# Column units gathered behind the row stage, one ring of five PSUM banks, a reordered start and zero products ahead of it

## The chip, the cores and the metric

The kernel runs on one core of one Trainium2 chip. Its time is device microseconds of one execution, taken as the median of several. The five engines of the core run their own instruction streams in order: TensorE (PE for matmuls, PEld for weight loads), VectorE (DVE), ScalarE (ACT), GpSimd (POOL) and SyncE (SP), which here only issues DMAs. An engine waits for another through semaphores.

## The reference

```python
# x: (8, 4224, 192), weight: (8 heads, 7 taps)
w = softmax(weight)                                  # per head
out = einsum('hk,bskhg->bshg', w, windows_of_7(x))   # causal convolution, one filter per head of 24 channels
# then, on that result x:
gate = sigmoid(sum_k conv_w[k] * shifted(x, k))      # causal, 5 taps per channel
val = x @ w_val                                      # 192 x 192
result = (gate * val) @ w_out                        # 192 x 192
```

## The kernel before

The tokens of the eight sequences are laid out as two long streams. They are cut into eleven groups `g`; `NJS` says how many windows of 122 tokens a group has per row (2, 4, eight times 6, and 2 at the end). A group is cut into column blocks of up to 458 tokens: the 39 steps `n` of the main loop. Steps 0 and 1 belong to group 0, steps 2 to 4 to group 1, and from step 5 on each full group has four steps.

**Column stage** (`conv_unit`, L277 and L286). The first convolution is a matmul: a load of input (`x<-xw`, one head of one group) is the stationary operand, `band` (a banded matrix of the softmaxed taps) the moving one. One unit is three or four of these matmuls into one PSUM bank `pc`, a ScalarE copy into a row buffer `e`, and, when the head of that group is complete, `conv_scatter`: DMAs that bring the rows into the channel-major tiles `x1` (channels 0 to 127, heads 0 to 4 and a part of 5; L303) and `x2` (channels 128 to 191, the rest of head 5 and heads 6 and 7; L318, four DMAs for one head). A full group has 16 units.

**Row stage**, per step `n`, on `x1` and `x2`:
- the gate: `gate_open` (ScalarE, L340) puts the first tap into the PSUM tiles `pa` (two banks) and `pb` (one bank), `gate_taps` (VectorE, L347) adds four more taps, `gate_close` (ScalarE, L360) writes the sigmoid to `g1` and `g2`. This runs one to two steps ahead.
- `split` (ScalarE casts L368 and L376, GpSimd subtractions L369 and L377) makes a high and a low half (`xh`, `xl`) of each operand, `split_gated1` and `split_gated2` the same (`ph`, `pl`) for the gated product.
- the product with `w_val`: `chunk1` (L398 to L400), `chunk21` (L408, 64 rows), `chunk12` (L415, 64 columns, float32), `chunk2` (L424), accumulated in `pv`. `gated(n, q)` (VectorE, L446) multiplies it with the gate: q = 0 and 1 are the halves of the first 128 channels, q = 2 the rest.
- the product with `w_out` for the step before (`o = n - 1`), the same four pieces into `po`, then `project` (ScalarE copies L461, one DMA per step).

The eight PSUM banks: `pa` 2, `pb` 1, four in turn for `pv` and `po`, and one, `ps_c`, for all column units. The order on every engine is the order in which the code is written (`manual_schedule`). In a step the column units stand in four places, `conv(c[0])` to `conv(c[3])`, one unit in each for a step with four; `due[n]` says how many must have been done. The beginning decodes the two weight matrices from 64-bit words on VectorE (`make`, L198 to L214; `low`, L244), does seven column units ahead of step 0, ten in step 0, five in step 1 and six in step 2, then four a step up to step 30 and one a step from 31 to 34.

## Time and profile before

| | us |
|---|---|
| median of three runs | 428.06 (427.2 to 428.23) |
| the profiled execution | 426.18 |
| span of its profile | 424.4 |
| matmuls busy (PE) | 387.3 (91%) |
| VectorE busy (DVE) | 351.4 (83%) |
| ScalarE busy (ACT) | 327.3 (77%) |
| GpSimd busy (POOL) | 235.5 (55%) |

The profile is of one execution. A row of the timeline begins with the start and the length in us; "x6" counts instructions that were merged into one row (a float32 matmul shows as two instructions, so a unit of three is x6), and the brackets say how long the engine had stood idle and what ended that. In a table of windows each engine has its busy time and, as x, its number of instructions. "SPq" is SyncE's instruction stream.

### The profile page before, as it was taken

What the parts mean: (1) busy time and instruction counts of PE and PEld (TensorE: products, weight loads), DVE (VectorE), ACT (ScalarE), POOL (GpSimd) and SP (SyncE); (2) the same over time, 40 slices, a digit from 0 to 9 for tenths busy, and PEclk for the clock granted to TensorE, in tenths of its full rate; (3) what the DMA queues carried; (4) which work ended last, traced back from release to release, by engine and by line L of the source; (5) the groups of instructions that cost most, each with busy time, mean ns of one, the idle gap of its engine ahead of it and who ended that gap; (6) DMA issues with size and microseconds to landing.
All of it is one profiled execution on the core that took longest, in us unless ns stands there. A gap on an engine that the chain in (4) does not pass through costs nothing.

```text
span 424.4 us, 7773 instructions
## 1 busy us (share of the span) xinstructions
PE 387.3 (91%) x2683; PEld 308.6 (73%) x2683; DVE 351.4 (83%) x466; ACT 327.3 (77%) x580; POOL 235.5 (55%) x170
## 2 busy tenths in 40 slices
PE   3437787999999999999999999999999999999897
PEld 3336666888877877777887888887787777776574
DVE  4855357799999899999998989999989998999980
ACT  4253466888888888888888888888888889888772
POOL 1322144565556666665666665556666666765770
PEclk9855899999999999999999999999999999999999
DMA  7572588788877788877877866887887766222313
GB/s 284 158 220 61 159 187 223 218 215 221 209 238 215 219 213 227 214 206 207 237 217 191 236 205 204 200 234 233 211 214 232 214 175 179 101 89 90 133 68 138
DMA packets 30819, 81.59 MB, mean 192 GB/s; under 512 B 4764, under 2 KB 9612, under 8 KB 30780
## 3 DMA queue, kind: packets, MB, share of 16 engines
q1 hardware_dynamic: 30524, 80.87, 67.8%
q8 instruction: 21, 0.34, 0.4%
q0 software_dynamic: 256, 0.24, 0.2%
q14 instruction: 18, 0.15, 0.1%
HBM read 28.85 MB, written 26.00 MB: 129 GB/s over the span
## 4 chain that ended last, share of the span: by engine, by line
PE 74%; DVE 10%; ACT 5%; DMA 4%; SPq 3%; issue 3%; POOL 1%; DVEq 0%; ACTq 0%; POOLq 0%
PE pc L277 23%; PE pv L415 7%; PE pv L408 6%; PE pv L424 6%; PE po L415 5%; PE po L408 5%; PE po L424 4%; DVE pa L347 4%; DVE pb L347 4%; PE po L398 3%; PE po L399 3%; PE po L400 3%; PE pv L398 3%; PE pv L399 3%; PE pv L400 3%
## 5 line engine op out<-in xcount | busy, mean ns | idle before, releaser
L347 DVE SCALAR_TENSOR_TENSOR pa<-x,cwt,pa 128x912 f32<-128x912 f32 (+6 forms) x156 | 175.4, 1124 | 23.4 <-ACT pa L340 16.1
L277 PEld LDWEIGHTS pc<-band,x 128*120 128x120 f32 x816 | 102.2, 186 | 30.2 <-ACT e L286 24.2
L277 PE MATMUL pc<-band,x 128*120 128x122 f32 x816 | 115.8, 279 | 7.6 <-ACT e L286 7.3
L286 ACT COPY e<-pc 120x366 f32<-120x366 f32 (+1 forms) x144 | 68.2, 475 | 68.8 <-PE pc L277 56.1
L347 DVE SCALAR_TENSOR_TENSOR pb<-x,cwt,pb 128x456 f32<-128x456 f32 (+6 forms) x156 | 105.0, 673 | 4.1
L369 POOL TENSOR_TENSOR pl<-g,ph 128x912 fp32r<-128x912 f32 (+5 forms) x38 | 79.2, 2085 | 50.2 <-ACT ph L368 50.2
L377 POOL TENSOR_TENSOR pl<-g,ph 128x456 fp32r<-128x456 f32 (+5 forms) x38 | 43.3, 1140 | 104.4 <-ACT ph L376 104.4
L446 DVE TENSOR_TENSOR g<-pv,g 128x456 f32<-128x456 f32 (+6 forms) x117 | 67.5, 604 | 31.9 <-PE pv L408 25.4
L369 POOL TENSOR_TENSOR xl<-x,xh 128x912 fp32r<-128x912 f32 (+6 forms) x39 | 71.2, 1826 | 15.9 <-ACT xh L368 15.9
L461 ACT COPY ot<-po 128x456 f32<-128x456 f32 (+6 forms) x117 | 57.5, 529 | 10.3 <-PE po L408 4.8
L415 PE MATMUL pv<-x,wvf 128*64 128x228 f32 (+6 forms) x312 | 37.8, 364 | 3.2 <-ACT ot L461 1.9
L398 PE MATMUL pv<-xh,wvh 128*128 128x456 f32 (+6 forms) x78 | 31.1, 399 | 10.2 <-ACT xh L368 10.2
L340 ACT ACTIVATE pa<-x,cwt 128x912 f32<-128x912 f32 (+6 forms) x39 | 38.8, 994 | 0.9 <-DMA x<-e 0.7
L377 POOL TENSOR_TENSOR xl<-x,xh 128x456 fp32r<-128x456 f32 (+6 forms) x39 | 39.3, 1007 | 0.0
L368 ACT CAST ph<-g 128x912 fp32r<-128x912 f32 (+5 forms) x38 | 36.1, 949 | 2.1 <-DVE g L446 2.1
L360 ACT ACTIVATE g<-pa 128x912 f32<-128x912 f32 (+6 forms) x39 | 35.7, 915 | 2.0 <-DVE pa L347 1.7
L368 ACT CAST xh<-x 128x912 fp32r<-128x912 f32 (+6 forms) x39 | 35.6, 914 | 0.0
L415 PE MATMUL po<-g,wof 128*64 128x228 f32 (+5 forms) x304 | 34.8, 349 | 0.0
L398 PE MATMUL po<-ph,woh 128*128 128x456 f32 (+5 forms) x76 | 30.8, 406 | 0.2 <-DVE g L446 0.2
L400 PE MATMUL pv<-xl,wvh 128*128 128x456 f32 (+6 forms) x78 | 28.6, 367 | 0.7 <-POOL xl L369 0.7
L399 PE MATMUL pv<-xh,wvl 128*128 128x456 f32 (+6 forms) x78 | 28.5, 365 | 0.0
L415 PEld LDWEIGHTS pv<-x,wvf 128*64 128x64 f32 x312 | 19.0, 138 | 12.5 <-ACT ot L461 2.8
(81 smaller groups left out, 580.1 us busy)
## 6 DMA issues: line engine op xcount, KB each, us to landing
x<-xw SPq DMA_DIRECT2D x64, 360.0 KB
out<-ot SPq DMA_DIRECT2D x24, 684.0 KB
x<-e SPq DMA_DIRECT2D x40, 343.1 KB
out<-ot SPq DMA_DIRECT2D x8, 687.0 KB
x<-e SPq DMA_DIRECT2D x32, 137.2 KB
x<-e SPq DMA_DIRECT2D x18, 114.4 KB
x<-e SPq DMA_DIRECT2D x20, 91.5 KB
stage<-xw SPq DMA_DIRECT2D x2, 720.0 KB
```

The source lines that it names most:

```text
L277: nc.tensor.matmul(pc[: NS * HC, n * WIN : (n + 1) * WIN], lhsT=xtiles[g, h][:, j * NS * HC : (j + 1) * NS * HC], rhs=band[:, h, :], start ...
L286: nc.scalar.copy(e[: NS * HC, o : o + n * WIN], pc[: NS * HC, : n * WIN])
L347: nc.vector.scalar_tensor_tensor(out=acc, in0=views(n, k)[i], scalar=cwt[:, i, k : k + 1], in1=acc, op0=ALU.mult, op1=ALU.add,)
L368: nc.scalar.copy(h, x)
L369: nc.gpsimd.tensor_tensor(out=l, in0=x, in1=h.bitcast(F32), op=ALU.subtract)
L377: nc.gpsimd.tensor_tensor(out=l, in0=x, in1=h.bitcast(F32), op=ALU.subtract)
L398: nc.tensor.matmul(acc, lhsT=w.h[:, r], rhs=h[:, q], start=True, stop=False)
L399: nc.tensor.matmul(acc, lhsT=w.l[:, r], rhs=h[:, q], start=False, stop=False)
L400: nc.tensor.matmul(acc, lhsT=w.h[:, r], rhs=l[:, q], start=False, stop=False)
L415: nc.tensor.matmul(acc[p, c], lhsT=w.f[:, W12 : W12 + 64], rhs=x1[:, q, c], start=(i == 0), stop=False)
L446: nc.vector.tensor_tensor(out=v, in0=pvs.pop((n, q)), in1=v, op=ALU.mult)
L461: nc.scalar.copy(ots[n][:, q * m : (q + 1) * m], acc)
```

## The change

- **Order of a step.** From step 2 on, all column units of a step stand behind its matmuls: `conv(min(todo, 1))`, `split_gated2`, then the rest. `chunk1` of both products, `chunk21` of both, `chunk12` of both and `chunk2` of both follow each other without units between them. VectorE has the four taps of `pa`, one of `pb`, `gated` 0 and 1, three of `pb`, `gated` 2 in a row.
- **One ring of banks.** `ps_c` is gone; `pv`, `po` and the units take turns in five banks.
- **The start.** All four units of group 0 and all eight of group 1 are done ahead of step 0; steps 0 and 1 have a loop of their own, with eight and four units at their ends. Six products of zeros (`ips<-idle`) stand at the head of TensorE's stream. The weights `wv` are loaded behind the first load of input instead of the second. The rows of groups 0 and 1 get tiles of pools that are not yet used (`rows`). The `x2` part of group 0 is sent by GpSimd, all `x1` parts by SyncE.
- **Order of the heads.** Heads 5, 6 and 7, which make `x2`, come first in each group (`HEADS`, `PAIRS`).

On TensorE, from the last matmul of `chunk21` to the end of the step (step 8; `pc` are column units, `x4` counts equal matmuls in a row), before:

```order
L408 MATMUL po_1_1287<-pl_7_1258,woh 128x456
L277 MATMUL pc_2_3_1308<-band,x_2_1013 120x122 x3
L415 MATMUL pv_2_1326<-x_2_380,wvf 64x228 x4
L415 MATMUL po_2_1331<-g_7_1095,wof 64x228 x4
L424 MATMUL pv_2_1326<-xh_8_1162,wvh 128x456
L424 MATMUL pv_2_1326<-xh_8_1162,wvl 128x456
L424 MATMUL pv_2_1326<-xl_8_1163,wvh 128x456
L277 MATMUL pc_3_0_1340<-band,x_3_1081 120x122 x3
L424 MATMUL po_2_1331<-ph_7_1257,woh 128x456
L424 MATMUL po_2_1331<-ph_7_1257,wol 128x456
L424 MATMUL po_2_1331<-pl_7_1258,woh 128x456
L277 MATMUL pc_3_3_1356<-band,x_3_1081 120x122 x3
```

and now, from `chunk12` of step 7 to that step's end:

```order
L434 MATMUL pv_2_1210<-x_2_385,wvf 64x228 x4
L434 MATMUL po_2_1215<-g_6_972,wof 64x228 x4
L443 MATMUL pv_2_1210<-xh_7_1065,wvh 128x456
L443 MATMUL pv_2_1210<-xh_7_1065,wvl 128x456
L443 MATMUL pv_2_1210<-xl_7_1066,wvh 128x456
L443 MATMUL po_2_1215<-ph_6_1129,woh 128x456
L443 MATMUL po_2_1215<-ph_6_1129,wol 128x456
L443 MATMUL po_2_1215<-pl_6_1130,woh 128x456
L296 MATMUL pc_5_0_1238<-band,x_5_928 120x122 x3
L296 MATMUL pc_5_3_1247<-band,x_5_928 120x122 x3
L296 MATMUL pc_6_0_1260<-band,x_6_1026 120x122 x3
L296 MATMUL pc_6_3_1265<-band,x_6_1026 120x122 x3
```

The four units of a step, which stood one by one between pieces of the products, now stand in one block. (The lines of the file moved: L277 is now L296, L398 L417, L408 L427, L415 L434, L424 L443, L347 L366, L446 L465.)

On TensorE in step 0, from the end of `chunk1` to the second product, before:

```order
L400 MATMUL pv_1_285<-xl_247,wvh 128x304
L277 MATMUL pc_3_0_304<-band,stage_97 120x122 x4
L277 MATMUL pc_4_0_312<-band,stage_97 120x122 x4
L277 MATMUL pc_5_0_320<-band,stage_97 120x122 x4
L408 MATMUL pv_0_284<-xh_0_250,wvh 128x304
```

and now:

```order
L296 MATMUL pc_4_0_292<-band,x_4_199 120x122 x4
L417 MATMUL pv_0_352<-xh_305,wvh 128x304
L418 MATMUL pv_0_352<-xh_305,wvl 128x304
L419 MATMUL pv_0_352<-xl_306,wvh 128x304
L417 MATMUL pv_1_353<-xh_305,wvh 128x304
L418 MATMUL pv_1_353<-xh_305,wvl 128x304
L419 MATMUL pv_1_353<-xl_306,wvh 128x304
L427 MATMUL pv_0_352<-xh_0_309,wvh 128x304
```

The three units of group 1 that stood ahead of `chunk21` of step 0 now stand ahead of its `chunk1`, and nothing stands between the two.

On VectorE, one step (`gated` of step 7 and the taps around it), before:

```order
L347 SCALAR_TENSOR_TENSOR pa_1116<-x_2_380,cwt,pa_1116 128x2x456 x3
L446 TENSOR_TENSOR g_7_1095<-pv_0_1147,g_7_1095 128x456
L446 TENSOR_TENSOR g_7_1095<-pv_1_1148,g_7_1095 128x456
L347 SCALAR_TENSOR_TENSOR pa_1116<-x_2_380,cwt,pa_1116 128x2x456
L347 SCALAR_TENSOR_TENSOR pb_1140<-x_2_381,cwt,pb_1140 128x456 x4
L446 TENSOR_TENSOR g_7_1138<-pv_2_1214,g_7_1138 128x456
```

and now:

```order
L366 SCALAR_TENSOR_TENSOR pa_1086<-x_2_385,cwt,pa_1086 128x2x456 x4
L366 SCALAR_TENSOR_TENSOR pb_1114<-x_2_386,cwt,pb_1114 128x456
L465 TENSOR_TENSOR g_7_1084<-pv_0_1155,g_7_1084 128x456
L465 TENSOR_TENSOR g_7_1084<-pv_1_1156,g_7_1084 128x456
L366 SCALAR_TENSOR_TENSOR pb_1114<-x_2_386,cwt,pb_1114 128x456 x3
L465 TENSOR_TENSOR g_7_1112<-pv_2_1210,g_7_1112 128x456
```

The same eleven instructions stand there; the fourth tap of `pa` and one tap of `pb` moved ahead of `gated` 0 and 1.

The core of the diff:

```diff
+HEADS = (5, 6, 7, 0, 1, 2, 3, 4)
+PAIRS = ((6, 7), (4, 5), (0, 1), (2, 3))
-    ps_c = ctx.enter_context(tc.tile_pool(name="ps_c", bufs=1, space=PSUM))
-    ps_v = ctx.enter_context(tc.tile_pool(name="ps_v", bufs=4, space=PSUM))
+    ps_v = ctx.enter_context(tc.tile_pool(name="ps_v", bufs=5, space=PSUM))
...
     load_x()
+    load_raw("wv")
     load_x()
-    load_raw("wv")
     load_raw("wo")
     load_x()
+    load_x()
+    idle = cp.tile([128, 256], F32, name="idle")
+    nc.gpsimd.memset(idle, 0.0)
+    ips = ps_v.tile([128, 512], F32, tag="pv", name="ips")
+    for _ in range(6):
+        nc.tensor.matmul(ips[:, :256], lhsT=idle[:, :128], rhs=idle, start=True, stop=True)
...
+    def rows(g, h):
+        name = f"e_{g}_{h}"
+        if g == 0 or g == 1 and h == 4:
+            t = pp.tile([128, 2, MB], F32R, tag="l" if g == 0 and h < 4 else "h", name=name)
+            return t.bitcast(F32).rearrange("p a t -> p (a t)")[:, :RUNM]
+        if g == 1 and 0 < h < 4:
+            t = gp.tile([128, 2, MB], F32, tag="g1", name=name)
+            return t.rearrange("p a t -> p (a t)")[:, :RUNM]
+        return ep.tile([128, RUNM], F32, tag="e", name=name)
...
-        queue = nc.gpsimd if g == 0 and h > X1 else nc.sync
+        queue = nc.sync
...
             n2 = HC - n1
+            queue = nc.gpsimd if g == 0 else nc.sync
...
+            if g == 2:
+                due[n] = (8, 12, 16)[min(n, 2)]
+                continue
...
-    conv(2, ps_v, "pv")
-    load_x()
-    conv(2, ps_v, "pv")
+    conv(count[0])
     for _ in range(XBUFS):
         load_x()
+    conv(4)
     w_val.make(NV)
-    w_val.low()
-    conv(3, ps_v, "pv")
+    conv(4)
     first_open(0)
     split(0)
+    w_val.low()
     w_out.make(NO)
+    split(1)
...
+    for n in range(EARLY, N):          # EARLY = 2
+        v1 = chunk1(w_val, n, *xs[n][:2], "pv")
+        o1 = chunk1(w_out, o, *ps[o, 1], "po")
+        gate_taps(n + 1, 0, 3, KG)
+        split(n + 1)
+        chunk21(w_val, v1, *xs[n][2:])
+        chunk21(w_out, o1, *ps[o, 2])
+        gate_taps(n + 1, 1, 1, 2)
+        gated(n, 0)
+        gated(n, 1)
+        gate_close(n + 1, 0)
+        gate_open(n + 2, 0)
+        project(o, 0, o1[0])
+        project(o, 1, o1[1])
+        split_gated1(n)
+        gate_taps(n + 1, 1, 2, KG)
+        v2 = chunk12(w_val, n, views(n)[0], "pv")
+        o2 = chunk12(w_out, o, g1s[o], "po")
+        chunk2(w_val, v2, *xs[n][2:])
+        gated(n, 2)
+        gate_close(n + 1, 1)
+        gate_open(n + 2, 1)
+        chunk2(w_out, o2, *ps[o, 2])
+        project(o, 2, o2)
+        gate_taps(n + 2, 0, 1, 3)
+        conv(min(todo, 1))
+        split_gated2(n)
+        conv(todo - min(todo, 1))
```

87 lines of the change are left out of this document (41 added, 46 removed).

## The prediction

> **What bounds the kernel now.** I read the page first, then a table of windows, then the timeline of one step in the middle and of the start. The page says that TensorE is busy nearly all the time, but not at the start:
>
> ```profile
> span 424.4 us, 7773 instructions
> PE 387.3 (91%) x2683; PEld 308.6 (73%) x2683; DVE 351.4 (83%) x466; ACT 327.3 (77%) x580; POOL 235.5 (55%) x170
> PE   3437787999999999999999999999999999999897
> DVE  4855357799999899999998989999989998999980
> DMA  7572588788877788877877866887887766222313
> ```
>
> Each digit is a slice of 10.6 us. The first eight slices, 85 us, are far from full on every engine; after that PE stands at 9 until the end. Two windows tell the middle from the end:
>
> ```profile
> 202.00:212.00 10.00, 10.00 (x72) 7.95 (x71) 9.04 (x12) 8.58 (x17) 6.55 (x4) 1.00 0.86 240
> 372.00:382.00 10.00, 9.38 (x66) 7.55 (x66) 9.82 (x14) 8.47 (x14) 6.11 (x5) 1.00 0.27 94
> ```
>
> The columns are PE, PEld, DVE, ACT, POOL, the granted clock, the DMA share and GB/s. In the middle PE has no idle time (10.00) and DVE has a tenth to spare; in the end, where the column units are done, DVE is the full one (9.82). So there are three regimes: a start in which nothing is full, 26 steps bound by TensorE, and a tail bound by VectorE. In the middle, one step on PE is this:
>
> ```profile
> 204.12 0.45 PE L398 MATMUL pv<-xh,wvh 128*128 128x456 f32 x1
> ...
> 205.45 0.79 PE L277 MATMUL pc<-band,x 128*120 128x122 f32 x6
> ...
> 206.00 0.45 PE L398 MATMUL po<-ph,woh 128*128 128x456 f32 x1
> ...
> 207.41 0.48 PE L408 MATMUL pv<-xh,wvh 64*128 64x456 f32 x2
> ...
> 208.84 0.89 PE L277 MATMUL pc<-band,x 128*120 128x122 f32 x6
> ...
> 209.67 0.99 PE L415 MATMUL pv<-x,wvf 128*64 128x228 f32 x8
> ...
> 211.36 0.47 PE L424 MATMUL pv<-xh,wvh 128*128 128x456 f32 x1
> ...
> 212.09 0.79 PE L277 MATMUL pc<-band,x 128*120 128x122 f32 x6
> ...
> 212.64 0.45 PE L424 MATMUL po<-ph,woh 128*128 128x456 f32 x1
> ...
> 213.43 0.89 PE L277 MATMUL pc<-band,x 128*120 128x122 f32 x6
> ...
> 214.08 0.46 PE L398 MATMUL pv<-xh,wvh 128*128 128x458 f32 x1
> ```
>
> I take the distance from one start to the next, since matmuls overlap and their lengths are modelled. The step is 9.96 us. The four units take 0.55, 0.83, 0.55 and 0.65, together 2.58; the rest is 1.33 + 1.41 + 1.43 + 1.69 + 0.73 + 0.79 = 7.38. The same unit costs 0.55 between two pieces of full 128 x 128 tiles and 0.83 between the 64-row pieces of L408 and the 64-column pieces of L415: what lies around a unit has a price.
>
> **The change part by part, the middle.** No matmul goes or comes there; only the order changes. Four units in one block at the good place cost 4 x 0.55 = 2.20, if their banks are free. In the rest, `chunk1` of the second product no longer follows a unit and `chunk2` of it neither. What they take without units around them is seen in the tail:
>
> ```profile
> 387.51 0.47 PE L424 MATMUL pv<-xh,wvh 128*128 128x456 f32 x1
> ...
> 388.86 0.37 PE L398 MATMUL pv<-xh,wvh 128*128 128x456 f32 x1
> ```
>
> Both `chunk2` in a row take 1.35 there, against 0.73 + 0.79 = 1.52 with a unit between: 0.17 less. I take 0.09 less for `chunk1`, half of that, as it is one edge and not two. New is the direct passage from L408 to L415, which the trace shows only in the tail, where L415 waits for VectorE. Its lower bound is 0 (1.43 for L408 has a passage to a unit in it already), its upper bound 0.28, what the unit at that place costs more than the others, if all of that is the passage and none of it the unit. I take 0.13, the middle, since no row is nearer to either. So the rest is 7.38 - 0.26 + 0.13 = 7.25 (7.12 to 7.40) and the step 9.45. For units in a row at full rate there is only the start (PE alone: its instructions as x, the granted clock, the DMA share, GB/s):
>
> ```profile
> 8.00:9.00 1.00, 1.00 (x7) 1.00 1.04 416
> 12.00:13.00 1.00, 1.00 (x12) 1.00 0.37 87
> 18.00:19.00 1.00, 0.00 (x0) 0.52 0.99 388
> ```
>
> At 12 instructions a us the 24 of four units take 2.0, my lower bound; the upper one is 2.6, all as the one of 0.65. The step's bounds are 9.1 to 10.0. A page of the Trainium skill speaks to that passage: TensorEngine Tiling (Array Packing), Key Properties, says that changing the tiling mode drains TensorE. By it, the order before changes mode four times a step (full, rows, full, columns, full) and the new one three times. With an estimate of 0.1 to 0.28 for a drain (at most the 0.83 less 0.55 of the unit at that place, which agrees in direction), the step by the page alone would be 9.68 to 9.86.
>
> Does another engine take over below 9.45? VectorE has the same eleven instructions. In the tail, where it is the bound, its step is the distance of these rows, 8.99:
>
> ```profile
> 376.46 1.17 DVE L446 TENSOR_TENSOR g<-pv,g 128x458 f32<-128x458 f32 x2
> ...
> 385.45 1.17 DVE L446 TENSOR_TENSOR g<-pv,g 128x456 f32<-128x456 f32 x2
> ```
>
> So it has 0.46 to spare. ScalarE's 8.58 of 10 becomes 8.55 of 9.45, 90%; the DMA share of 0.86 becomes 0.91. Waits for banks: each step takes ten turns in five banks, and a unit's bank is freed by a copy of 0.475 (the groups of the page):
>
> ```profile
> L286 ACT COPY e<-pc 120x366 f32<-120x366 f32 (+1 forms) x144 | 68.2, 475 | 68.8 <-PE pc L277 56.1
> ```
>
> `po` 2 needs the bank that `gated` 0 frees, the units those of `gated` 1, the two copies of `project` and `gated` 2, the next step's `pv` and `po` those of the third `project` and of the units' copies. The nearest is the last: the copies of units two to four, 0.475 each behind the second cast of the gated product, end about 1.2 us into the next step, and the banks are used by `chunk1` of the second product, from 1.3 us on, and by `chunk12`. By my estimate the others come half a us or more ahead. The rows of heads 3 and 4 arrive last in a group, about when `pa` of the next group is opened; a ScalarE wait of up to 1 us there has no follower on PE. I count these at nothing; the cover is the 0.46 of DVE and the tenth of ACT, and if it is gone, each us late costs a us per step.
>
> Steps 5 to 30 have four units: 26 x (9.96 - 9.45) = 13.3 us less. For the tail I count nothing, since the order of the same DVE work sets it.
>
> **The start.** Before, VectorE stands still for other engines in steps 0 to 2:
>
> ```profile
> 19.54 0.85 DVE L214 TENSOR_TENSOR wof<-scr,scr 128x320 f32<-128x320 f32 x3
> ...
> 24.13 3.53 DVE L347 SCALAR_TENSOR_TENSOR pa<-x,cwt,pa 128x608 f32<-128x608 f32 x4 [3.73 <-ACT pa L340]
> ...
> 27.69 0.62 DVE L244 TENSOR_TENSOR wol<-wof,woh 128x448 fp32r<-128x448 f32 x1
> ...
> 28.23 2.26 DVE L347 SCALAR_TENSOR_TENSOR pb<-x,cwt,pb 128x304 f32<-128x304 f32 x4
> ...
> 39.22 0.86 DVE L446 TENSOR_TENSOR g<-pv,g 128x304 f32<-128x304 f32 x2 [4.96 <-PE pv L408]
> ...
> 59.83 2.68 DVE L347 SCALAR_TENSOR_TENSOR pb<-x,cwt,pb 128x406 f32<-128x406 f32 x4
> ...
> 63.10 3.28 DVE L347 SCALAR_TENSOR_TENSOR pa<-x,cwt,pa 128x812 f32<-128x812 f32 x3 [0.21 <-ACT pa L340]
> ...
> 69.32 1.07 DVE L446 TENSOR_TENSOR g<-pv,g 128x406 f32<-128x406 f32 x2 [2.95 <-PE pv L408]
> ...
> 98.75 1.18 DVE L446 TENSOR_TENSOR g<-pv,g 128x458 f32<-128x458 f32 x2 [0.31 <-PE pv L408]
> ```
>
> The pairs of `gated` 0 and 1 of steps 0, 2 and 5 start at 39.22, 69.32 and 98.75. Step 0 waits because `chunk21` stands behind three units, whose tiles and copies are late. With all twelve units ahead, the new start is a chain on DVE. What can hold its first link, the opening of `pa`, is the rows of group 0 and ScalarE's place behind the copies of the units:
>
> ```profile
> 9.64 4.89 POOL L318 DMA_DIRECT2D x<-e  x8 [8.18 <-ACT e L286]
> ...
> 16.00 3.39 SPq L303 DMA_DIRECT2D x<-e  x4
> ...
> 18.62 4.60 DMA x<-e
> ...
> 19.44 2.41 SPq L135 DMA_DIRECT2D x<-xw  x5
> ```
>
> SyncE needs 0.85 to issue a row DMA and 0.48 for a load; GpSimd 0.61. From the first copy that SyncE can send, at about 9, six `x1` issues end at 14 and two loads for the last units at 15. They land by 17 to 19.5 (the 4.60 above, in a full queue, is the upper bound; I take half), their units and copies end by 18.5 to 20, and `pa` is open by 19.5 to 21. GpSimd's twelve (eight before) end at 9 + 7.3 = 16.3 and are hidden. The decoding of the weights ends at 19.54 + 0.85 = 20.4, as before, since the cast between its two halves stands behind the copies; so the taps start at about 20.4 instead of 24.13. From there: `pa` 3.53, `wol` 0.62, `pb` 2.26, three `gated` 1.3 (28.1); step 1's taps, of nearly the same size, 3.53 + 2.26 (33.9). TensorE is then still in the eight units of group 2: SyncE has 16 row issues and four loads to send from 15 on, 15.5 us, before the last of their inputs, which lands at about 33; two units and the products to L408 end at 36. So a wait of 2.1, three `gated` with the wait for the third 2.2 (38.2), `pa` 4 x 1.09 = 4.37, `pb` 2.68, the next `pa` 4.37, a tap of `pb` 0.67: step 2's `gated` at 50.3 instead of 69.32, 19.0 earlier. The three steps to step 5 took 29.4 and would take 8.65 (DVE: 1.07 + 2.01 + 0.54 + 4.37 + 0.67), 9.1 (between the two) and 9.45, 2.2 less. Together 21.2. Bounds: 15, if the first taps and the wait at step 1 are 3 us later each, to 25, if step 1 does not wait and the rows are early.
>
> The zero products, the second load order and the tiles for the first rows act ahead of 20.4 and are hidden by the decoding; I count them at nothing, and up to 1 us if the cast comes earlier. What the products may do beyond is raise and keep the clock: in the three windows above, the units went at 7 instructions a us at first and at 12 later, and the clock fell to 0.52 three us after the last unit at 15.
>
> **The sum.** 424.4 - 21.2 - 13.3 = 389.9 of span. The profiled execution was 426.18, 1.8 above its span: 391.7. The median of the runs, 428.06, was 1.9 above that execution: 393.5.
>
> **The rivals.**
> 1. *The middle does not shorten.* A second engine is late in each step by the little that is gained: ScalarE at 90%, or the passage L408 to L415 at its dear end and units at 0.65. For it: ACT's copies follow four units at once. Against: ACT has 1.4 idle in 10. The step is then 9.9 and the time 405.
> 2. *The start gives half.* The DMAs queue (share near 1 in the row at 18 to 19 us), or TensorE is slow: at 7 instructions a us, the eight units of step 0 (48 instructions) take 6.9 instead of 4.0, and the products as much longer, 5 us. The time is 404. The Trainium skill, TensorE: Matmul & The Clock Gate, the part on the warm-up, says that the clock starts at half rate, rises after about 3.4 us of sustained work and falls after an idle window as long. By that rule the six products (an estimated 12 instructions of 0.3) fill just one window, so that they may or may not raise the clock before the first unit; the rows at 8, 12 and 18 us agree with both times.
> 3. *VectorE binds everywhere.* If the block of units and the passage are at their cheap ends, the step is 9.0, DVE's: 26 x 0.96 = 25.0 instead of 13.3, and the time 382.
> 4. *Slower: the units wait for each other's banks.* Before, two units in a row waited like this:
>
> ```profile
> 48.44 0.89 PE L277 MATMUL pc<-band,x 128*120 128x122 f32 x6 [0.55 <-ACT e L286]
> ```
>
> If the ring gives each of the four units such a wait because ScalarE is behind, the step is 9.45 + 2.2 = 11.65 and the time 393.5 + 26 x 2.2 = 451. It decides where the waits pass (428.06 - 393.5) / 26 = 1.33 us a step. Against it: five banks in place of one, and the releases as laid out above.
>
> **How the numbers follow.** The forecast, start and middle both as summed, has 0.60, with its own range from 385 to 402 (15 to 25 for the start, steps of 9.3 to 9.65). Rival 1 has 0.16, rival 2 0.12, rival 3 0.06, rival 4 0.05, and 0.01 is left for no change. The range 384 to 408 leaves out rivals 3 and 4 and both of 1 and 2 at once (416). A measurement of this kernel tells about 0.3% from no change: faster by more 0.94, within it 0.01, slower 0.05.
>
> **What would show it.** Right: `gated` of step 2 at 47 to 54 and of step 5 at 74 to 82; four units on PE within 2.0 to 2.4 us and the step at 9.3 to 9.65; PE's wait for ACT, DVE or copies in the middle under 0.2 a step; the tail still at 9.0 on DVE. Wrong: a PE row at L296 or L434 with a wait for a copy in each step, DVE waiting longer than 0.7 a step for PE, ACT full; or steps 0 and 1 ending on the landing of rows or loads.

## The result, and the profile after

The changed kernel is slower: 455.39 us median of four runs (451.95 to 459.5), against 428.14 (427.2 to 430.21) for the kernel before on the same chip. The ratio is 1.060, with a 95% interval from 1.051 to 1.069. Here and below a median is of all runs of a kernel, while a ratio leaves out, on both sides, those more than 1.5% above the kernel's fastest. The forecast was 393.5. The profiled execution took 451.95 us, its span is 450.2. Its page begins so (busy time, and slices of 11.3 us):

```profile
span 450.2 us, 7807 instructions
...
PE   7767776999599969996999599959995999799897
DMA  8949784788378837883998398839982877332323
```

Before, PE stood at 9 in every slice of the middle. Now there is a slice of 5 or 6 every four slices, with a 2 or 3 beside it in the DMA row. Four slices are 45 us, which is about four steps, and four steps are one group. So something happens once per group. The table of waits names it (engine, line and tile waited for: us in total, times, longest):

```profile
ACT pa L359 <- DMA x<-e: 49.1, 8, 8.0
DVE pa L366 <- ACT pa L359: 36.4, 9, 5.2
PE pc L296 <- ACT ot L480: 31.5, 7, 5.2
...
ACT pa L359 <- issue: 7.4, 1, 7.4
```

Nine times ScalarE waits at L359, the opening of `pa`, 56.5 us in all. Eight of these waits, one at the first step of each full group, last 4.7 to 8.0 us, 7.0 in the mean; the ninth is 0.4. All but one are put down to row transfers (`x<-e`); for that one, 7.4 us in group 2, the table names nothing ("issue"), but it stands at the same place of its group. Behind the opening stand VectorE, which needs `pa`, and TensorE, which needs the banks that ScalarE empties. The timeline of one such place, at the change from one group to the next ("SPq" rows are SyncE sending DMAs):

```profile
197.31 0.35 SPq L485 DMA_DIRECT2D out<-ot  x1
...
197.75 0.38 SPq L137 DMA_DIRECT2D x<-xw  x1
...
198.50 0.78 SPq L321 DMA_DIRECT2D x<-e  x1
...
199.38 0.50 SPq L137 DMA_DIRECT2D x<-xw  x1
...
199.99 1.82 SPq L321 DMA_DIRECT2D x<-e  x1
...
205.31 0.79 PE L296 MATMUL pc<-band,x 128*120 128x122 f32 x6
208.46 1.03 ACT L359 ACTIVATE pa<-x,cwt 128x916 f32<-128x916 f32 x1 [6.70 <-DMA x<-e]
209.42 0.97 ACT L480 COPY ot<-po 128x456 f32<-128x456 f32 x2
209.52 4.81 DVE L366 SCALAR_TENSOR_TENSOR pa<-x,cwt,pa 128x916 f32<-128x916 f32 x4 [3.92 <-ACT pa L359]
210.01 3.34 PE L296 MATMUL pc<-band,x 128*120 128x122 f32 x18 [3.91 <-ACT ot L480]
```

From 197.3 to 201.8 SyncE sends, in a burst, an output (684 KB, of 1024 bytes), a load (360), the rows of head 3 (343), a load (360) and the rows of head 4 (343): 2,090 KB. The last rows are sent from 199.99 to 201.81 and the opening that needs them starts at 208.46. ScalarE stands for 6.70 us; `project`'s copies stand behind it, so PE gets through one more unit and stops in its block. What the DMA engines did meanwhile (columns: PE, PEld, DVE, ACT, POOL, granted clock, DMA share, GB/s):

```profile
199.00:201.00 2.00, 2.00 (x12) 1.55 (x12) 1.97 (x3) 1.72 (x4) 1.29 (x2) 1.00 0.98 292
201.00:203.00 2.00, 2.00 (x20) 1.46 (x22) 1.50 (x4) 0.76 (x1) 1.90 (x2) 1.00 1.07 244
203.00:205.00 2.00, 2.00 (x17) 1.43 (x14) 1.93 (x5) 0.00 (x0) 0.00 (x0) 1.00 0.72 172
205.00:207.00 2.00, 1.10 (x9) 0.87 (x7) 0.60 (x2) 0.00 (x0) 0.00 (x0) 1.00 0.76 190
207.00:209.00 2.00, 0.00 (x0) 0.00 (x0) 0.00 (x0) 0.54 (x1) 0.00 (x0) 1.00 0.06 12
```

They work through the burst until about 207, then have nothing to do, and the opening starts 1.5 us later: the rows land with the last bytes of the burst, or just behind them. The share at its end is 0.72 to 0.76; 12 of 16 engines would be 0.75. The Trainium skill, DMA: Bandwidth & Descriptors, the paragraph on how many engines a transfer uses, says that it is the largest number up to 16 which divides the slowest dimension on both sides; for rows of 120 partitions written to 24, that is 12. The share in this place agrees; no row tells the engines apart.

The steps between are short: the `gated` pairs at 138.65, 148.24 and 157.83 are 9.59 us apart. The table has the starts of these pairs in the timelines, and the distance of steps 5 to 30 divided by 25; the forecast's step 0 is 28.1 - 1.3, its step 5 98.75 - 21.2, its step 30 that and 25 x 9.45:

| kernel | step 0 | step 2 | step 5 | step 30 | a step | span |
|---|---|---|---|---|---|---|
| before | 39.22 | 69.32 | 98.75 | 348.24 | 9.98 | 424.4 |
| forecast | 26.8 | 50.3 | 77.6 | 313.8 | 9.45 | 389.9 |
| after | 35.85 | 58.79 | 93.26 | 372.37 | 11.16 | 450.2 |

The span is 60.3 us longer than forecast. Of that 15.7 are lost by step 5, 42.9 between steps 5 and 30, 1.7 behind.

### The profile page after: what moved, and what is told of

Same layout as the page of the kernel before. It is cut to its first block, busy times and chain, and to the rows that moved or that the text cites. A ratio compares the mean times of both kernels' runs of the same rounds, so it can differ in the third digit from the quotient of the medians.

```text
span 450.2 us, 7807 instructions
## 1 busy us (share of the span) xinstructions
PE 392.2 (87%) x2695; PEld 323.8 (72%) x2695; DVE 350.8 (78%) x466; ACT 328.3 (73%) x580; POOL 239.1 (53%) x175
## 4 chain that ended last, share of the span: by engine, by line
PE 46%; DMA 15%; DVE 12%; ACT 6%; issue 5%; POOL 1%; ACTq 0%; SPq 0%; DVEq 0%; POOLq 0%
DMA x<-e 14%; PE pc L296 14%; DVE pa L366 6%; PE pv L427 4%; PE pv L434 3%; PE pv L443 3%; DVE pb L366 3%; PE po L434 3%; DVE g L465 3%; PE po L443 2%; PE po L419 2%; PE po L427 2%; PE pv L417 2%; PE pv L418 2%; PE po L417 2%
## 5 line engine op out<-in xcount | busy, mean ns | idle before, releaser
L366 DVE SCALAR_TENSOR_TENSOR pa<-x,cwt,pa 128x912 f32<-128x912 f32 (+6 forms) x156 | 175.5, 1125 | 40.6 <-ACT pa L359 36.4
L296 PE MATMUL pc<-band,x 128*120 128x122 f32 x816 | 109.1, 296 | 37.0 <-ACT ot L480 31.5
L296 PEld LDWEIGHTS pc<-band,x 128*120 128x120 f32 x816 | 106.9, 210 | 39.9 <-ACT ot L480 32.8
L366 DVE SCALAR_TENSOR_TENSOR pb<-x,cwt,pb 128x456 f32<-128x456 f32 (+6 forms) x156 | 104.6, 671 | 2.9
L465 DVE TENSOR_TENSOR g<-pv,g 128x456 f32<-128x456 f32 (+6 forms) x117 | 67.5, 604 | 40.8 <-PE pv L427 31.2
L359 ACT ACTIVATE pa<-x,cwt 128x912 f32<-128x912 f32 (+6 forms) x39 | 38.6, 989 | 57.4 <-DMA x<-e 49.1
L305 ACT COPY e<-pc 120x366 f32<-120x366 f32 (+1 forms) x144 | 62.7, 488 | 11.9 <-PE pc L296 10.1
L480 ACT COPY ot<-po 128x456 f32<-128x456 f32 (+6 forms) x117 | 56.5, 516 | 7.7 <-PE po L454 2.9
L396 POOL TENSOR_TENSOR pl<-g,ph 128x456 fp32r<-128x456 f32 (+5 forms) x38 | 43.5, 1144 | 28.1 <-ACT ph L395 24.8
L434 PE MATMUL po<-g,wof 128*64 128x228 f32 (+5 forms) x304 | 35.5, 355 | 6.9 <-DVE g L465 6.9
L434 PE MATMUL pv<-x,wvf 128*64 128x228 f32 (+6 forms) x312 | 37.8, 364 | 0.0
L387 ACT CAST xh<-x 128x912 fp32r<-128x912 f32 (+6 forms) x39 | 36.9, 946 | 0.0
L417 PE MATMUL pv<-xh,wvh 128*128 128x456 f32 (+6 forms) x78 | 32.6, 418 | 4.1 <-ACT xh L387 2.4
L434 PEld LDWEIGHTS po<-g,wof 128*64 128x64 f32 x304 | 21.4, 138 | 15.0 <-DVE g L465 8.5
L379 ACT ACTIVATE g<-pb 128x456 f32<-128x456 f32 (+6 forms) x39 | 20.9, 535 | 15.3 <-DVE pb L366 15.2
L419 PE MATMUL po<-pl,woh 128*128 128x456 f32 (+5 forms) x76 | 27.9, 367 | 2.8 <-POOL pl L388 2.6
```

Of the source, the lines that this page charges most:

```text
L296: nc.tensor.matmul(pc[: NS * HC, n * WIN : (n + 1) * WIN], lhsT=xtiles[g, h][:, j * NS * HC : (j + 1) * NS * HC], rhs=band[:, h, :], start ...
L305: nc.scalar.copy(e[: NS * HC, o : o + n * WIN], pc[: NS * HC, : n * WIN])
L366: nc.vector.scalar_tensor_tensor(out=acc, in0=views(n, k)[i], scalar=cwt[:, i, k : k + 1], in1=acc, op0=ALU.mult, op1=ALU.add,)
L379: nc.scalar.activation(dst, accs.pop((n, i)), AF.Sigmoid)
L387: nc.scalar.copy(h, x)
L396: nc.gpsimd.tensor_tensor(out=l, in0=x, in1=h.bitcast(F32), op=ALU.subtract)
```

## The experiments

Theory L: the rows of heads 3 and 4 land too late for the opening of `pa`, once a group, and this is the loss in the middle. Its main rival R was the prediction's fourth case, units that wait in each step for banks that ScalarE has not emptied. Where nothing else is said, a kernel differs from the changed one by the edit shown alone, and ratios are to the kernel before.

**Units one step earlier.** `CB` says how many steps ahead of a group's first step its units are to be done.

```
-CB = 2
+CB = 3
```

> CB = 3 in place of 2: from group 3 on, all convolution units of a group are done one step earlier; number and order of all other instructions stay. Theory L (late rows): ScalarE opens `pa` of a group's first step half a step after the last row transfer was sent, and this transfer lands 7 to 9 us after its sending. Then the 8 waits of ScalarE at L359 for `x<-e` go (49.1 us in the changed kernel, under 8 here), a group takes 4 x 9.5 = 38 us where it takes 44.6, and the time is 455 - 8 x 6 = 407 us (400 to 415). Rival R (the ring of five banks with a ScalarE that is behind in every step, the prediction's fourth case): moving units by a step changes nothing in a step's work, so 450 to 458 us. Rival B (the loads that share the queue are what is late): the rows' wait goes but PE then waits for `x<-xw`, 430 to 445 us.

Measured: 412.15 us, ratio 0.959 (0.955 to 0.963). Theory L holds, R falls. The opening waits for rows only once more, in group 2, whose units CB does not move; and the window from 200 to 210 us, where the hole was, has no idle time of PE left:

```profile
ACT pa L359 <- DMA x<-e: 5.9, 1, 5.9
```

```profile
200.00:210.00 10.00, 10.00 (x74) 8.33 (x73) 9.35 (x12) 9.07 (x17) 7.06 (x5) 1.00 0.88 247
```

A step is 9.59 us. The 25 steps from 5 to 30 take 239.7, not 279.1: 39.4 of the 42.9 us lost there.

**The order of the heads.**

```
-LOADS += [(_g, (_h,)) for _g in range(2, NG - 1) for _h in HEADS]
+LOADS += [(_g, (_h,)) for _g in range(2, NG - 1) for _h in range(NH)]
...
-        for hs in PAIRS if nj == 2 else [(h,) for h in HEADS]:
+        for hs in PAIRS if nj == 2 else [(h,) for h in (HEADS if g < 2 else range(NH))]:
```

> From group 2 on the heads are taken in the order 0 to 7 as in the kernel before, where the changed kernel takes 5, 6, 7, 0, ..., 4; the prologue is left as it is. Now the rows of heads 6 and 7, which feed only chunk 2, are the last. Theory L: `pa` needs the rows of heads 0 to 5 alone, which land a step earlier, so its waits at L359 go; the opening of `pb`, half a step later, waits instead for 8 small transfers that SP sends one after another, 0 to 4 us a group: 455 - 8 x 4 = 423 us (405 to 440). Rival (the order plays no part, since whatever is sent last in the burst is late by the same): 450 to 458 us with the wait at `pb`.

Measured: 421.52 us, ratio 0.979 (0.974 to 0.984). With the old order the same kernel takes 2.1% less than before (1.6 to 2.6%), where the changed one takes 6.0% more. So it is the new order of the heads, together with the lead of `CB = 2`, that made the change slower. What is left is a smaller wait, at the opening of `pb`, further on in the step:

```profile
ACT pb L359 <- DMA x<-e: 20.5, 8, 3.0
```

The opening of `pb` stands 4.0 us behind that of `pa` (192.19 and 196.17 in a step of the changed kernel without a wait), and these 4.0 us are more than half of the 7.0 that were missing.

**Why the rows take so long.** Three runs, on the place in the queue, the queue itself, and the bytes. First, the rows ahead of the load instead of behind it:

```
+            for i, h in enumerate(hs):
+                conv_scatter(g, h, e[:, i * run : (i + 1) * run])
             if loaded[0] < len(LOADS) and LOADS[loaded[0] - XBUFS] == (g, hs):
                 load_x()
-            for i, h in enumerate(hs):
-                conv_scatter(g, h, e[:, i * run : (i + 1) * run])
```

> In conv_unit the rows of a head are sent before the next load of x, not behind it, so one load of 360 KB less stands between the last unit of a group and its last row transfer. Theory L in the form that the row transfer stands in line behind what SP sent before it (an output of 684 KB, two loads of 360 KB and the rows of head 3): the wait shortens by what one load takes, 1.5 to 2 us, 8 times: 455 - 14 = 441 us (436 to 447), the waits at L359 from 49 to 33-40 us. Rival: the landing time of 7 to 9 us is a fixed latency of such a transfer: 453 to 457 us, waits 47 to 50. Rival R (ring of banks): no change either.

Measured: 446.63 us, ratio 1.037 (1.030 to 1.044): 8.8 us less, at the far end of what theory L allowed in this form.

```profile
ACT pa L359 <- DMA x<-xw: 31.8, 5, 8.2
...
ACT pa L359 <- DMA x<-e: 17.6, 4, 6.2
```

The sum at L359 is 49.4, where it was 56.5: 7.1 less and not 9 to 16. Five of nine waits are now put down to the load that was sent behind the rows, though the opening does not read it. Counted from the end of SyncE's sending to the start of the opening, the last rows take 6.0 to 9.2 us, 7.1 in the mean of eight groups; in the changed kernel they take 6.2 to 8.2, 7.2 in the mean. The place ahead of the load did not make them land sooner; they are only sent sooner. Next, the output in another queue, which takes no byte out of the burst:

```
-            nc.sync.dma_start(out[:, o : o + 3 * m], ots[n][:, : 3 * m])
+            nc.scalar.dma_start(out[:, o : o + 3 * m], ots[n][:, : 3 * m])
```

> The changed kernel with only this: each step's output (684 KB) is issued by ScalarE, in a queue of its own, and no longer by SyncE ahead of the two loads and the rows. Theory Q (the rows stand in line in SyncE's queue behind the output): the landing of the last rows comes earlier by most of what 684 KB take at 230 GB/s, 3.0 us, at 8 groups: waits at L359 25 to 30 us instead of 49, time 455 - 8 x 3 = 431 us. Rival V (the burst as a whole has to go through the same 16 DMA engines, and a second queue only shares them): waits 45 to 52 us, 452 to 458 us.

```profile
ACT pa L359 <- DMA x<-e: 29.5, 5, 9.1
ACT pa L359 <- issue: 27.7, 4, 9.6
```

Measured: 457.45 us, ratio 1.063 (1.059 to 1.066), and 57.2 us of waiting at L359 (four of the nine are put down to "issue", as was one before). No change: theory Q falls. The Trainium skill, DMA: Bandwidth & Descriptors, the section on issuing engines that are not separate queues, says that transfers run on the same 16 engines and interleave, whoever issued them; this run agrees. Last, the two loads out of the burst, sent by ScalarE behind the opening:

```
-                load_x()
+                if g > 1 and hs in ((3,), (4,)):
+                    later[0] += 1
+                else:
+                    load_x()
...
         gate_open(n + 2, 0)
+        while later[0]:
+            later[0] -= 1
+            load_x(nc.scalar)
```

> The changed kernel with only this: the two loads of x (360 KB each) that go with the last rows of a group are issued by ScalarE behind the opening of the next `pa`, so they leave the burst. What is left in it is the output and the rows, 1.37 MB instead of 2.09 MB. Theory V (the rows are late by the bytes of the burst): 0.72 MB less at 230 GB/s is 3.1 us less of waiting at 8 groups, 455 - 25 = 430 us, waits at L359 25 to 30 us. Theory Q gives about the same, since both loads stood ahead of the last rows. Rival T (such a row transfer takes 7 to 9 us by itself, whatever else is moved): no change, 452 to 458 us. A third way: the loads come too late instead and PE waits for `x<-xw`, above 455 us.

```profile
ACT pa L364 <- DMA x<-e: 38.4, 9, 7.4
```

Measured: 429.98 us, ratio 0.998 (0.995 to 1.001), where 430 was expected. That the time came out is partly luck: the waits fell by 18 us, not 25, and the two profiled executions differ by 20.6 us where the medians differ by 25. T, no change at all, falls. But the bytes are only a part of it. From the last copy of a unit to the opening it took 9.5 us in the mean of eight groups and takes 7.2 here. Of these 2.3 us, 1.3 come from SyncE, which has the rows sent sooner when no load stands between, and 1.0 from the landing: 6.2 us behind the sending (5.2 to 8.4) and not 7.2. Theory V asked for 3.1 from the bytes alone. So most of the landing stays when 720 KB leave the burst, and what it consists of is open: no run sent the rows alone.

```profile
199.77 2.15 PE L298 MATMUL pc<-band,x 128*120 128x122 f32 x18 [2.95 <-ACT ot L485]
```

A shorter wait is also worth more than its length. PE stands 2.95 us here, and its next 18 instructions take 2.15 us at a granted clock of 1.00; in the changed kernel it stands 3.91, and they take 3.34, the clock being 0.50 from 211 to 214 us.

**What the step of 9.59 is made of.** Two runs with CB = 3, so without the late rows. The first sets the four units apart again:

```
+        c = [todo // 4 + (i < todo % 4) for i in (0, 2, 1, 3)]
         v1 = chunk1(w_val, n, *xs[n][:2], "pv")
+        conv(c[0])
         o1 = chunk1(w_out, o, *ps[o, 1], "po")
...
         gate_open(n + 2, 0)
+        conv(c[1])
...
         gate_open(n + 2, 1)
+        conv(c[2])
         chunk2(w_out, o2, *ps[o, 2])
...
-        conv(min(todo, 1))
         split_gated2(n)
-        conv(todo - min(todo, 1))
+        conv(c[3])
```

> CB = 3, and in the steps from 2 on the four units stand apart again, one behind chunk1 of the first product, one behind chunk21, one behind the first chunk2, one at the end, as in the kernel before; the five banks stay. Theory B (what shortens a step is the block: 9.59 us against 9.96 to 9.98 with the units apart): 412 + 25 x 0.38 = 422 us, steps of 9.9 to 10.0. Rival F (the fifth common bank shortens it by taking waits away, and where the units stand is all the same): 411 to 414 us, steps of 9.55 to 9.65.

Measured: 414.73 us, ratio 0.967 (0.962 to 0.973); a step 9.79. Neither theory is right. Of the 0.39 us that a step is shorter than before, half is the block (9.79 to 9.59). The other half (9.98 to 9.79) stands at the last unit of a step, 0.65 before and 0.55 here, and the product ahead of it, 0.79 before and 0.69 here; whether the bank or the new place of other engines' work is its cause was not tried. The time is only 2.6 us above the 412.15 and not 25 x 0.2 = 5; in the profiles the start makes up for it, with step 5 at 93.47 and not 97.50. PE with the units apart, and then in a block (the step of the run with CB = 3):

```profile
201.24 0.89 PE L296 MATMUL pc<-band,x 128*120 128x122 f32 x6
202.06 0.99 PE L434 MATMUL pv<-x,wvf 128*64 128x228 f32 x8
...
204.49 0.79 PE L296 MATMUL pc<-band,x 128*120 128x122 f32 x6
205.04 0.45 PE L443 MATMUL po<-ph,woh 128*128 128x456 f32 x1
205.33 0.36 PE L443 MATMUL po<-ph,wol 128*128 128x456 f32 x1
...
205.73 0.79 PE L296 MATMUL pc<-band,x 128*120 128x122 f32 x6
206.28 0.46 PE L417 MATMUL pv<-xh,wvh 128*128 128x458 f32 x1
```

```profile
206.33 2.68 PE L296 MATMUL pc<-band,x 128*120 128x122 f32 x24
208.77 0.45 PE L417 MATMUL pv<-xh,wvh 128*128 128x458 f32 x1
...
212.38 0.37 PE L427 MATMUL po<-ph,wol 64*128 64x456 f32 x2
212.59 0.37 PE L427 MATMUL po<-pl,woh 64*128 64x456 f32 x2
212.89 1.00 PE L434 MATMUL pv<-x,wvf 128*64 128x228 f32 x8
```

Four units in a block take 208.77 - 206.33 = 2.44; apart they take 0.82 once and 0.55 three times, 2.47. The block saves nothing on the units. It saves on the products: the first one behind a unit takes 0.29 (205.04 to 205.33), the next 0.20. Each place where one kind of work follows another costs some 0.09, and the block has two such places fewer: 0.18 and 0.03 are the 0.2 of the step.

The second run gives the units one bank of their own, and the products four:

```
-    ps_v = ctx.enter_context(tc.tile_pool(name="ps_v", bufs=5, space=PSUM))
+    ps_v = ctx.enter_context(tc.tile_pool(name="ps_v", bufs=4, space=PSUM))
+    ps_c = ctx.enter_context(tc.tile_pool(name="ps_c", bufs=1, space=PSUM))
...
-        pc = ps_v.tile([128, 512], F32, tag="pv", name=f"pc_{g}_{hs[0]}_{j0}")
+        pool, tag = (ps_c, "pc") if own[0] else (ps_v, "pv")
+        pc = pool.tile([128, 512], F32, tag=tag, name=f"pc_{g}_{hs[0]}_{j0}")
...
+    own[0] = True
     for n in range(EARLY, N):
```

> CB = 3, units in a block, but from step 2 on in one bank of their own with four for the products, as in the kernel before. Theory: the common pool is what makes the block possible; in one bank the second, third and fourth unit each wait for the copy of the one ahead, 0.55 us as in the kernel before where two stood in a row, or up to 0.8: 412 + 26 x (1.65 to 2.4) = 455 to 474 us. Rival: PE makes the waits up, since VectorE would be next at 9.0 us and the products run ahead: 412 to 425 us.

```profile
176.75 0.79 PE L299 MATMUL pc<-band,x 128*120 128x122 f32 x6
178.46 0.89 PE L299 MATMUL pc<-band,x 128*120 128x122 f32 x6 [0.92 <-ACT e L308]
179.91 0.89 PE L299 MATMUL pc<-band,x 128*120 128x122 f32 x6 [0.55 <-ACT e L308]
```

Measured: 510.6 us, ratio 1.188 (1.179 to 1.196). The profiled execution took 517.27 us; only the waits are read from it, at a place where the granted clock was 1.00. The mechanism is the one expected, its price about twice as high: a unit starts 1.45 to 1.71 after the one ahead, not 0.61 (2.44 / 4). The time is 98 us more over 26 steps, 3.8 a step, where 1.65 to 2.4 were expected. The common pool is what makes the block possible.

**The start.** Without the zero products:

```
-    for _ in range(6):
+    for _ in range(0):
```

> The six products of zeros ahead of the first convolution unit are left out. The prediction counted them at nothing, 0 to 1 us: 455 to 457 us. Rival (they give the first units a fast TensorE clock): units of groups 0 and 1 run at the lower rate of the kernel before, 7 rather than 12 a us, from 7 us on for some 4 us, so that the first gated products come about 2 us later, and so does the end: 457 to 459 us.

Measured: 455.96 us, ratio 1.063 (1.057 to 1.069): no difference from 455.39 that could be told. The rival was right on the rate and wrong on the time. Without the zero products the units run at 7 instructions a us from 8 to 12 us, with them at 12. But the last two units of group 1 wait for their x either way: they come after 1.92 us of idle time here and take 1.91 us, after 3.11 us with the zero products and take 3.47, and the first taps even start earlier, at 23.44 and not 24.63. Next, CB = 3 and the old order of heads at once:

> CB = 3 and heads 0 to 7 in order from group 2 on, both edits that brought time back singly. Theory L (late rows, at the start too): group 2 is not moved by CB, so its rows still come late in the run with CB = 3 alone (step 5 opens its gated pair at 97.5 us there, at 87.5 in the run with the heads in order). With both, the start is that of the second and the steps those of the first, 9.59 us: 412 - 10 = 402 us (399 to 407). Rival: the start of the run with CB = 3 is late because step 2 has eight units instead of four, not for its rows; then the order brings nothing more, 410 to 413 us.

Measured: 407.03 us, ratio 0.948 (0.943 to 0.953). That is the edge of the range: 5.1 of the 10 us came in the medians. In the profile step 5 opens at 89.61, between the 87.51 and 97.50 of the single edits. Then, on top of that:

```
-            queue = nc.gpsimd if g == 0 else nc.sync
+            queue = nc.gpsimd if g <= 1 else nc.sync
```

> As the run before, and the small row transfers of heads 5, 6 and 7 in group 1 (twelve, 11.0 us of SyncE in the changed kernel from 18.4 to 29.4 us) are issued by GpSimd, which stands idle from 16.7 to 25.8 us there. Theory S: the first sigmoid waited 7.7 us because its tile still held rows of group 1 that SyncE had not sent behind those twelve; with them gone, the first gated pair starts at 32 to 33 us and not at 35.9, and step 5 and the end come 3 us earlier: 399 us if the run before has 402, always 2 to 4 us below it. Rival: the start hangs on the loads and rows of group 2 or on TensorE's slow clock, and the gain at the first gate is given back by step 3: within 1 us of the run before.

Measured: 406.29 us, ratio 0.945 (0.939 to 0.951). In the trace step 0 comes 4.3 us earlier, step 2 2.6, step 5 2.3; in the medians, 0.7, nothing can be told. Inconclusive on the time. The start in the timeline of the changed kernel, and one row of the same place in this run:

```profile
19.80 3.47 PE L296 MATMUL pc<-band,x 128*120 128x122 f32 x16 [3.11 <-DMA x<-xw]
...
24.63 3.53 DVE L366 SCALAR_TENSOR_TENSOR pa<-x,cwt,pa 128x608 f32<-128x608 f32 x4 [2.91 <-ACT pa L359]
...
28.19 1.78 DVE L254 TENSOR_TENSOR wol<-wof,woh 128x448 fp32r<-128x448 f32 x1
...
35.14 0.68 ACT L379 ACTIVATE g<-pa 128x608 f32<-128x608 f32 x1 [7.74 <-DMA x<-e]
35.85 0.85 DVE L465 TENSOR_TENSOR g<-pv,g 128x304 f32<-128x304 f32 x2 [3.72 <-ACT g L379]
```

```profile
32.07 0.68 ACT L379 ACTIVATE g<-pa 128x608 f32<-128x608 f32 x1 [3.98 <-DMA x<-e]
```

Four runs on this base. Zero products again, but where PE stands idle for x ahead of the last two units of group 1:

```
-    conv(4)
+    conv(2)
+    ips2 = ps_v.tile([128, 512], F32, tag="pv", name="ips2")
+    for _ in range(5):
+        nc.tensor.matmul(ips2[:, :256], lhsT=idle[:, :128], rhs=idle, start=True, stop=True)
+    conv(2)
     first_open(0)
```

> As the run with the rows of group 1 by GpSimd, with five more products of zeros (128 x 256, results unused) ahead of the last two units of group 1, where TensorE stood idle for 3 us waiting for x and then ran these units at a granted clock of 0.5: 16 instructions in 3.5 us. Theory C (the slow clock after an idle stretch is what delays the first taps): the 16 take 1.4 us, `pa` opens and the first taps start 2 us earlier (25.3 to 23.3 us), the first gated pair 1.5 to 2 us earlier (32.8 to 31), and the end 1 to 2 us earlier, 404 to 405 us where the run before had 406.3. Rival: the rest of the start is set by the transfers (DMA share near 1 from 18 to 52 us), the gain is gone by step 2: within 1 us of 406.

```profile
17.72 2.33 PE L525 MATMUL ips<-idle 128*128 128x256 f32 x10
...
21.08 1.91 PE L296 MATMUL pc<-band,x 128*120 128x122 f32 x16 [1.02 <-DMA x<-xw]
```

The windows in which these units run, here and in the changed kernel (the clock is the third number from the right):

```profile
21.00:22.00 1.00, 0.92 (x9) 0.95 (x10) 0.93 (x3) 0.00 (x0) 1.00 (x3) 1.00 0.95 271
```

```profile
20.00:21.00 1.00, 1.00 (x6) 1.00 (x7) 0.93 (x3) 0.00 (x0) 0.00 (x0) 0.50 0.99 368
```

Measured: 403.76 us, ratio 0.939 (0.936 to 0.941). Theory C is right on the clock: the 16 instructions take 1.91 us (it asked for 1.4), not the 3.47 of the changed kernel or the 3.56 of the run this one builds on. But in this profile the sigmoid waited 8.4 us for rows, and step 0 was no earlier (36.27). That the 2.5 us of the medians come from the clock is not shown. Then the last units of group 2 a step earlier, `due` (8, 16, 16) for (8, 12, 16), alone and with the zero products:

> As the run with the rows of group 1 by GpSimd, but the last four units of group 2 stand at the end of step 1 instead of step 2, so that step 2 has four units (of group 3) and not eight; there VectorE waited 3.8 us for TensorE. Theory P (TensorE stands idle from 53.8 to 57.5 us and is full from then on; 2.5 us of units moved ahead of the gap fill it): step 5 opens at 85 and not at 87.3 us, the time is 404 us. Rival D (the transfers set the start; the units come no earlier since their x and their row tiles do not): 406 to 408 us, and PE or ScalarE wait for `x<-xw` or `x<-e` in step 1.

> Both edits of the two runs before together. If theories C and P both hold: 402 us. If the transfers set the start: 405 to 408 us.

Measured: 408.71 us, ratio 0.951 (0.949 to 0.954), and 409.45 us, ratio 0.952 (0.948 to 0.955). P falls, and rival D has the waits that it asked for, though both times are just above its range: in the first, up to 100 us, PE waited 6.2 us for `x<-xw` and ScalarE's copies 8.7 for `x<-e` (3.2 and 4.0 in the run they build on), and step 2 opened at 65.56, not 56.86. Last, with the zero products, the rows of group 1 out of the gate's tiles:

```
-XBUFS, EBUFS = 5, 4
+XBUFS, EBUFS = 5, 7
...
-        if g == 1 and 0 < h < 4:
+        if False:
```

> As the run with zero products in the gap, but the rows of heads 1 to 3 of group 1 stand in three more tiles of the pool `ep` (seven buffers instead of four) and no longer in the tiles of the gate. Theory S (the first sigmoid waits because its tile holds rows that are not yet sent: 7.7 us in the changed kernel, 4.0 and 8.4 in the two runs before): the wait goes, the first gated pair starts at 31 to 32.5 us instead of 32.8 to 36.3, and as the later row tiles come free sooner too, the time is 2 to 4 us less than the 403.8 of the run before: 400 to 402 us. Rival D (the transfers set the start, so the row tiles only move the wait to the first copies of group 2 or to the opening of step 2): the first gated pair comes earlier, step 5 does not (87 to 91 us), 403 to 406 us.

```profile
26.82 0.68 ACT L379 ACTIVATE g<-pa 128x608 f32<-128x608 f32 x1 [0.79 <-DVE pa L366]
...
68.30 1.07 DVE L465 TENSOR_TENSOR g<-pv,g 128x406 f32<-128x406 f32 x2 [4.25 <-PE pv L427]
```

Measured: 403.04 us, ratio 0.941 (0.938 to 0.945). The wait is gone and step 0 opens at 31.38, so theory S names the right cause of that wait; but the time is that of the run with the zero products alone, as rival D said; step 5 is at 86.27, against 90.99 in that run and 87.27 in the one ahead of both. Rival D's reason, the transfers, does not show between 44 and 88 us: there TensorE, VectorE and ScalarE wait for a transfer for 0.3 us at most. VectorE's long wait, the second row, is for TensorE. TensorE had stood for 5.93 us, up to 56.02, behind VectorE, whose taps of the next `pa` come ahead of `gated` from step 2 on; then the eight units of step 2 took 6.05 us, the granted clock being 0.50 to 0.55 from 57 to 61, where two blocks of four take 4.88. These two kernels are the fastest of the study, 6.1 and 5.9% below the kernel before, and cannot be told from each other.

## Why the prediction was wrong

**The step that failed.** "The rows of heads 3 and 4 arrive last in a group, about when `pa` of the next group is opened; a ScalarE wait of up to 1 us there has no follower on PE. I count these at nothing." The place was right, its size and its followers were not. The wait was 7.0 us in the mean of eight groups, 8.0 at most, and both VectorE and PE stood behind it. For the start I had priced the sending and a landing (4.60 us "in a full queue"), but neither at a group's end, where the rows land 6.2 to 8.2 us behind their sending. Figures that I had at hand would have warned: 2,090 KB sent together, at the 240 GB/s of the window at 202 us, are 8.9 us; as an account of the landing this is too simple, as the run without the two loads shows. And the words "no follower on PE" overlooked that the copies of `project` stand behind the opening on ScalarE and hold the banks of the units: PE waited 31.5 us for them.

**The middle otherwise.** Forecast 9.45, bounds 9.1 to 10.0, own range 9.3 to 9.65; without late rows it is 9.58 to 9.59 in every run that keeps the block and the five banks. Units in a block: forecast 2.20, measured 2.44, the term that is off. The rest: forecast 7.25, measured 9.59 - 2.44 = 7.15. The passage from L427 to L434 costs 0.30 - 0.21 = 0.09, forecast 0.13. With the drains of the Trainium skill's TensorEngine Tiling (Array Packing), Key Properties, my estimate was 9.68 to 9.86; the trace has 0.09 for this change of mode, and 0.09 too for a product behind a unit, where the mode stays. A drain with a price of its own isn't seen here. Of the 13.3 us forecast for the middle, 10.1 would come without the late rows (26 x 0.39).

**The start.** Forecast 21.2 earlier at step 5, bounds 15 to 25; it is 5.5 in the changed kernel, and 11.5, 7.8 and 12.5 in the runs with the rows of group 1 by GpSimd, with the zero products in the gap, and with the rows out of the gate's tiles. The terms: the first taps at 24.63, not 20.4, since the last two units of group 1 wait 3.11 for x and then run at a clock of 0.50. This was named as rival 2, and was partly right. `wol` took 1.78 us, not 0.62. The first `gated` waited for a sigmoid whose tile, one of the tiles "for the first rows" counted at nothing, still held rows that had not been sent on: ScalarE waited 7.74 for them, VectorE 3.72 for it. From `gated` 1 to `gated` 2 the sum held (14.3 against 14.3). The rest, 7.2 up to step 5, is the wait at the opening of group 2's `pa` (7.4), the same error as in the middle. Even without these waits step 5 stays at 86 to 87, not 77.6. In the last run 5.1 of these 8.7 us are there by step 2 (55.39), and what sets them is open; the other 3.6 come with VectorE's wait of 4.25 behind the eight units.

**The rest.** The tail holds (9.0 on VectorE). Zero products at nothing: right for the time, but not because they are hidden; they take 5.2 us (estimated 3.6), they raise the rate of the first units, and TensorE then waits the longer for x. Rival 4 gave 451 and the time came near it by luck: it asked for a wait in each step, and the first experiment excludes it. The rivals had no case of late rows, and the chance of 0.05 for slower was too small for that reason: among the things counted at nothing, none was asked what it would cost if its cover were gone for more than a us. By its own bounds the forecast's range would end at 405, not at 402 (15 for the start, steps of 9.65); that changes nothing here.

## What to carry to other kernels

When a step is moved nearer to the work that reads its transfer, price its landing and not only its sending, and put that beside the lead that is left. All bytes that are on their way at that moment, divided by the rate that a window shows, is a first estimate; here it gave the size, but not what fewer bytes would save. A wait that looks private to one engine is shared by all that stands behind it on that engine: list the banks and tiles that it holds. If a table of waits shows a wait once per group, look at the lead first: one more step removed it here, fewer bytes in the burst took a third off, and a second queue changed nothing.

## What the runs showed of the hardware

- A 343 KB transfer sent last in a burst of 2,090 KB landed 6.2 to 8.2 us behind the end of its sending; with one load of 360 KB behind it instead of ahead 6.0 to 9.2 us, and with both loads out of the burst 5.2 to 8.4 us.
- A stall of PE costs more than its length when it is long enough. After 3.91 us the granted clock was 0.50 from 211 to 214 us, and 18 instructions took 3.34 us; after 2.95 us, in the run without the two loads, it was 1.00 and they took 2.15. At the start it was 0.50 after a stall of 3.11 us, and five zero products in that gap kept it at 1.00. PE had stopped at 16.7 us there and the mean of 19 to 20 us is 0.81, so the clock fell about 2.9 us after the stop. The Trainium skill, TensorE: Matmul & The Clock Gate, the part on the warm-up, has the clock fall after an idle window of some 3.4 us; the trace has it somewhat sooner.
- A granted clock of 1.00 does not say that PE is at its full rate: from 8 to 9 us it is 1.00 both in the changed kernel and in the one without the zero products, and PE does 12 instructions of the units in the first and 7 in the second. What holds the rate down is not in these rows.
- VectorE's `wol`, started at 28.19 while a GpSimd subtraction ran (28.02 to 29.49), took 1.78 us, and 0.62 in the kernel before without one. In the run with the rows out of the gate's tiles it started 0.06 us ahead of such a subtraction: it took 0.63, and the subtraction 1.90 and not 1.48. The one that came second was the longer.
